# A spectral filter plus a gated MLP on one core: a task list by earliest positions, evacuations on ScalarE, one group's fix on VectorE, finer first loads, and down projections last

## The chip, the cores and the metric

The kernel runs on one core of a Trainium2 chip. The metric is the device time of one launch in microseconds (us), the median over several launches. Every run was also traced, so each has a *span* (first to last instruction), which is about 2 us shorter than the device time of the same run.

Runs that were sent together ran on one chip, interleaved with runs of the kernel before, and are compared with those. On chips 2 and 5 every kernel, the one before included, lost 10 to 18 us more in its first 31 us or so (the kernel before about 14 us, by its times). No number from such a chip is set against a number from another chip without saying so.

## The reference

```python
def reference(A_x, A_w_r, A_w_i, B_x, B_w_gate, B_w_up, B_w_down):   # B_x is not used
    x  = A_x                                  # [1, 2048, 512] bf16
    xn = layernorm(x)                         # over the 512 columns
    spec = irfft2(rfft2(xn) * (w_r + 1j*w_i)) # over 2048 x 512
    h    = gelu_tanh(xn @ w_gate) * (xn @ w_up)   # 512 -> 1792
    return x + spec + h @ w_down              # 1792 -> 512
```

Both transforms are done as matrix products. So TensorE has two streams of work: the gated MLP ("GLU": gate and up products, then down products), and a spectral chain of short steps, each of which this kernel copies out of PSUM before the next starts (such a copy of [128 x 512] takes 0.60 us on ScalarE in the changed kernel).

## The kernel before

The sequence is 16 chunks of 128 rows. GLU work comes in 56 units (4 blocks of 512 rows, 14 column slices). The spectral work is a list of tasks that are dealt out evenly between the units. The steps have short names, by the tile that they write: `tp` transposes of normalised x, `bp` first column step, `dp` row step, `ep` second column step, then the filter on VectorE, `gp` the inverse column step, `yp` the inverse row step, and `y_ps` the down products. A scheduler in the framework may move instructions a little within an engine's queue; the order used below is the one that the traces show.

The parts that matter here (cuts marked with `...`):

```python
def evac(o, i):                       # PSUM -> SBUF copies of bp, dp, gp
    flip[0] ^= 1
    if flip[0]: nc.scalar.copy(out=o, in_=i)
    else:       nc.vector.tensor_copy(out=o, in_=i)

def filt(g):                          # one of 8 groups
    V = nc.vector
    ...                               # ten VectorE operations, [128 x 512] or [128 x 1024], two of them [128 x 4] copies
    if g == 0:                        # one partition of group 0 needs a real-valued fix
        G = nc.gpsimd
        G.tensor_tensor(out=u[:, 0], in0=E0[:, :, 0], in1=TR0, op=ALU.mult)   # [1 x 512]
        ...                           # seven such operations, the last one tiny

def glu(sb, fc):
    ...                               # 4 gate and 4 up matmuls of 512 columns
    nc.scalar.activation(out=ge[:], in_=gp[:], func=AF.Gelu_apprx_tanh)
    nc.vector.tensor_tensor(out=hT[sb][:, fc, :], in0=up[:], in1=ge[:], op=ALU.mult)
    # gate and up PSUM tiles: two buffers each

layernorm(0)                          # chunks 0 to 3, rsqrt by 12 small VectorE operations
transposes(0)
tasks = []                            # ... layernorm, transposes, fold, bp for all chunks
for g in range(NG + 3):
    if g < NG:           tasks += [dstep(g, 0), dstep(g, 1)]      # as lambdas
    if 1 <= g < NG + 1:  tasks += [cstep(g - 1) and filt(g - 1)]
    if g >= 3:           tasks += [icstep(g - 3)]
# tasks dealt out evenly over 41 units; down(0..3) before unit 42, down(4..15) at the end
```

Of the kernel before, what the change touches and what calls it, by code (L numbers as in the profile page):

```python
# [10 lines left out]
P = 128  # L11
BF16 = mybir.dt.bfloat16
F32 = mybir.dt.float32
I32 = mybir.dt.int32
ALU = mybir.AluOpType
AF = mybir.ActivationFunctionType

S = 2048
D = 512
NC = 16  # L20
NG = 8
NE = 4
# [131 lines left out]
def kernel(  # L154
# [34 lines left out]
    Bs = pc.tile([P, 4, 2, NG, NC, 8], BF16, name="Bs", tag="Bs")  # L189
    RF_t = pc.tile([P, NC, P], BF16, name="RF_t", tag="RF")  # L190
    late = {}
    TR = pc.tile([P, NG, 2, 258], BF16, name="TR")
    TI = pc.tile([P, NG, 2, 258], BF16, name="TI")

    def cc(name, shape=None):
        o, w = ccols[name]
# [2 lines left out]
    def load_consts(first, last):  # L199
        a, b = ccols[first][0], sum(ccols[last])  # L200
        nc.sync.dma_start(out=CT[:, a:b], in_=cap[:, a:b])


    nc.sync.dma_start(out=x_t[:, 0:2, :], in_=x_v[:, 0:2, :])
    nc.sync.dma_start(out=x_t[:, 2:4, :], in_=x_v[:, 2:4, :])
    load_consts("ident", "ident")
    FCH = [(0, 256), (256, 768), (768, 1280), (1280, 1792)]
    fa, fb = FCH[0]
    nc.sync.dma_start(out=Wg_sb[:, :, fa:fb], in_=wg_v[:, :, fa:fb])
    nc.sync.dma_start(out=Wu_sb[:, :, fa:fb], in_=wu_v[:, :, fa:fb])  # L210
    nc.sync.dma_start(out=x_t[:, 4:8, :], in_=x_v[:, 4:8, :])
    nc.sync.dma_start(out=RF_t[:], in_=rf_d.rearrange("p (c k) -> p c k", c=NC))
    for fa, fb in FCH[1:]:
        nc.sync.dma_start(out=Wg_sb[:, :, fa:fb], in_=wg_v[:, :, fa:fb])
        nc.sync.dma_start(out=Wu_sb[:, :, fa:fb], in_=wu_v[:, :, fa:fb])
        if fa == 256:
            nc.sync.dma_start(out=x_t[:, 8:12, :], in_=x_v[:, 8:12, :])
            nc.sync.dma_start(out=x_t[:, 12:16, :], in_=x_v[:, 12:16, :])
            load_consts("F0", "F3")
    load_consts("I0", "M20")  # L220


# [23 lines left out]
    nc.gpsimd.memset(xn[:, :, D:D + 2], 0.0)  # L246


    def rsqrt(y, var):

        V = nc.vector
        v = pw.tile([P, 4], F32, name="v")
        t = pw.tile([P, 4], F32, name="t")
        V.tensor_scalar(out=v[:], in0=var, scalar1=EPS, scalar2=None, op0=ALU.add)
        vi, ti, yi = v[:].bitcast(I32), t[:].bitcast(I32), y[:].bitcast(I32)
        V.tensor_scalar(out=ti, in0=vi, scalar1=1, scalar2=None, op0=ALU.logical_shift_right)
        V.tensor_scalar(out=yi, in0=ti, scalar1=-1, scalar2=0x5F3759DF, op0=ALU.mult, op1=ALU.add)
        for _ in range(3):
            V.tensor_tensor(out=t[:], in0=y[:], in1=y[:], op=ALU.mult)
            V.scalar_tensor_tensor(out=t[:], in0=v[:], scalar=-0.5, in1=t[:],  # L260
                                   op0=ALU.mult, op1=ALU.mult)
            V.scalar_tensor_tensor(out=y[:], in0=t[:], scalar=1.5, in1=y[:],
                                   op0=ALU.add, op1=ALU.mult)

    def layernorm(cg):
        c0 = 4 * cg
        stats = pw.tile([P, 4, nc.vector.BN_STATS_DIM], F32, name="stats")
        mv = pw.tile([P, 4, nc.vector.BN_AGGR_DIM], F32, name="mv")
        rstd = pw.tile([P, 4], F32, name="rstd")
        for j in range(4):  # L270
            nc.vector.bn_stats(out=stats[:, j, :], in_=x_t[:, c0 + j, :])  # L271
            nc.vector.bn_aggr(out=mv[:, j, :], in_=stats[:, j, :])
        rsqrt(rstd, mv[:, :, 1])
        for j in range(4):
            nc.vector.tensor_scalar(out=xn[:, c0 + j, 0:D], in0=x_t[:, c0 + j, :],  # L275
                                    scalar1=mv[:, j, 0:1], scalar2=rstd[:, j:j + 1],
                                    op0=ALU.subtract, op1=ALU.mult)

    def transposes(cg):
        for h in range(2):  # L280
            c0 = 4 * cg + 2 * h
            tp = ps.tile([P, NE, 2, P], BF16, name="tp", tag="S", bufs=4)
            for e in range(NE):
                for j in range(2):
                    nc.tensor.transpose(tp[:, e, j, :], xn[:, c0 + j, e * P:(e + 1) * P], ident)  # L285
            if h == 0:
                nc.vector.tensor_copy(out=xnT[:, :, c0:c0 + 2, :], in_=tp[:])
            else:
                nc.scalar.copy(out=xnT[:, :, c0:c0 + 2, :], in_=tp[:])  # L289


    fold_out = {}
# [19 lines left out]
    def pstep(cg, q):  # L312
        xf = fold_out[cg]
        bp = ps.tile([P, 4, 2 * NG, 8], F32, name="bp", tag="S", bufs=4)
        for j in range(4):
            nc.tensor.matmul(bp[:, j], lhsT=xf[:, j, q, :], rhs=RF_t[:, 4 * cg + j, :],  # L316
                             start=True, stop=True)
        o = Bs[:, q].rearrange("p r g c a -> p c (r g) a")[:, 4 * cg:4 * cg + 4]
        evac(o, bp[:])

    flip = [0]

    def evac(o, i):
        flip[0] ^= 1
        if flip[0]:
            nc.scalar.copy(out=o, in_=i)
        else:
            nc.vector.tensor_copy(out=o, in_=i)

    ds_tiles = {}  # L330

# [41 lines left out]
    def filt(g):  # L373
# [21 lines left out]
        if g == 0:  # L395

            u = pw.tile([1, 2, 2, 256], BF16, name="u", bufs=1)
            G = nc.gpsimd
            E0, F0 = E[0:1], F[0:1]
            TR0, TI0 = TR[0:1, 0, :, 0:256], TI[0:1, 0, :, 0:256]  # L400
            G.tensor_tensor(out=u[:, 0], in0=E0[:, :, 0], in1=TR0, op=ALU.mult)
            G.tensor_tensor(out=u[:, 1], in0=E0[:, :, 1], in1=TI0, op=ALU.mult)
            G.tensor_tensor(out=F0[:, 0], in0=u[:, 0], in1=u[:, 1], op=ALU.add)
            G.tensor_tensor(out=u[:, 0], in0=E0[:, :, 1], in1=TR0, op=ALU.mult)
            G.tensor_tensor(out=u[:, 1], in0=E0[:, :, 0], in1=TI0, op=ALU.mult)
            G.tensor_tensor(out=F0[:, 1], in0=u[:, 0], in1=u[:, 1], op=ALU.subtract)
            G.tensor_tensor(out=F0[:, :, :, 0], in0=E0[:, :, :, 0].rearrange("p r s -> p s r"),  # L407
                            in1=f_tiles["t0"][:], op=ALU.mult)
# [49 lines left out]

    hT = {}

    def glu(sb, fc):
        if fc == 0:
            tag = ("hT0", "hT1", "xn", "hT0")[sb]
            hT[sb] = pc.tile([P, NFC, 512], BF16, name=f"hT{sb}", tag=tag)
        rhs = xnT[:, :, 4 * sb:4 * sb + 4, :].rearrange("p e c q -> p e (c q)")
        gp = ps.tile([P, 512], F32, name="g_ps", tag="G", bufs=2)
        up = ps.tile([P, 512], F32, name="u_ps", tag="U", bufs=2)
        for e in range(NE):
            nc.tensor.matmul(gp[:], lhsT=Wg_sb[:, e, fc * P:(fc + 1) * P], rhs=rhs[:, e, :],  # L469
                             start=(e == 0), stop=(e == NE - 1))  # L470
        for e in range(NE):
            nc.tensor.matmul(up[:], lhsT=Wu_sb[:, e, fc * P:(fc + 1) * P], rhs=rhs[:, e, :],  # L472
                             start=(e == 0), stop=(e == NE - 1))
        ge = pw.tile([P, 512], BF16, name="ge", bufs=3)
        nc.scalar.activation(out=ge[:], in_=gp[:], func=AF.Gelu_apprx_tanh)  # L475
        nc.vector.tensor_tensor(out=hT[sb][:, fc, :], in0=up[:], in1=ge[:], op=ALU.mult)  # L476

    def down(c):
        sb, cl = c // 4, c % 4
# [8 lines left out]
        nc.sync.dma_start(out=out_v[:, c, :], in_=y_sb[:])  # L488


    layernorm(0)
    transposes(0)
    tasks = []
    for cg in range(1, 4):
        tasks.append(lambda cg=cg: layernorm(cg))
        tasks.append(lambda cg=cg: transposes(cg))
    for cg in range(4):
        tasks.append(lambda cg=cg: fold(cg))
        for q in range(4):
            tasks.append(lambda cg=cg, q=q: pstep(cg, q))  # L500
    tasks.append(tables_fix)
    for g in range(NG + 3):
        if g < NG:
            tasks.append(lambda g=g: dstep(g, 0))
            tasks.append(lambda g=g: dstep(g, 1))
        if 1 <= g < NG + 1:
            tasks.append(lambda g=g: (cstep(g - 1), filt(g - 1)))
        if g >= 3:
            tasks.append(lambda g=g: icstep(g - 3))
    for c in range(NC):  # L510
        tasks.append(lambda c=c: idstep(c))
    units = [(sb, fc) for sb in range(NSB) for fc in range(NFC)]
    ti = 0
    SPAN = 41
    for i, u in enumerate(units):
        if i == 3 * NFC:
            while ti < len(tasks):
                tasks[ti]()
                ti += 1
            for c in range(4):  # L520
                down(c)
        glu(*u)
        target = (i + 1) * len(tasks) // SPAN
        while ti < min(target, len(tasks)):
            tasks[ti]()
            ti += 1
    for c in range(4, NC):
        down(c)


# [28 lines left out]
```

## Time and profile before

| | |
|---|---|
| device time | 209.67 us, median of 3 (209.47 to 210.68) |
| span of the profiled run | 208.9 us (a fourth run, which took 211.05 us) |
| TensorE busy | 187.7 us, 90% of the span |
| all matmuls at their full-speed spacing | about 180 us (an estimate) |
| first transpose / first gate matmul | 10.55 / 13.80 us |

The estimate in the fourth line takes the spacing that full-speed groups show in the timeline (about 0.060 us for 128 columns, 0.110 for 256, 0.216 for 512) times the number of matmuls. TensorE is therefore the engine that bounds the kernel, and what can be won is the time in which it stands still or runs slowly.

From the page of the kernel before: busy time of the engines, then the span in 40 slices of 5.2 us, then the chain of waits by engine.

```profile
span 208.9 us, 2903 instructions
...
PE 187.7 (90%) x1040; PEld 94.3 (45%) x1040; DVE 140.3 (67%) x360; ACT 71.5 (34%) x118; POOL 30.3 (15%) x41
...
PE   0079999999999199999999999999999999999992
...
DVE  2998999999779979999995999323433312212121
...
PEclk9999999999999759999999999999999999999998
...
PE 74%; DVE 13%; POOL 3%; DMA 3%; issue 2%; ACT 2%; SPq 1%; POOLq 0%; DVEq 0%
```

The PE row has two holes: the first two slices and slice 14 (about 68 to 73 us), and the granted clock dips just there and after. VectorE (DVE) is almost full until about 130 us, with a dip at 110 to 115 us, and 10 to 40% busy after that.

The waits of TensorE in the kernel before, longest first: who waited for whom, us in total, times, longest.

```profile
PE tp L285 <- DVE xn L275: 10.6, 1, 10.6
PE gp L422 <- POOL F L407: 4.8, 1, 4.8
PE g_ps L469 <- ACT xnT L289: 1.1, 1, 1.1
PE gp L422 <- DVE F L393: 0.4, 1, 0.4
```

The timeline of TensorE around the second hole, in the kernel before: start, duration of the group, instructions, and in brackets the idle time before it with what ended it.

```profile
72.56 1.89 PE L422 MATMUL gp<-CT,F 128*128 128x256 bf16 x8 [4.84 <-POOL F L407]
74.24 0.74 PE L336 MATMUL dp<-CT,Bs 128*128 128x129 bf16 x4
74.78 1.91 PE L469 MATMUL g_ps<-xnT,Wg_sb 128*128 128x512 bf16 x4
...
79.09 1.03 PE L469 MATMUL g_ps<-xnT,Wg_sb 128*128 128x512 bf16 x4
```

Four gate matmuls of the same shape take 1.91 us after the hole and 1.03 us about four microseconds later (the record of a group ends after the next group has started, at 80.12 against 79.95 us for the later one, so read starts: 74.78 to 76.48 is 1.70 us, 79.09 to 79.95 in the same trace is 0.86 us). TensorE ran at half speed after the pause: the clock records of the packed trace put it at half speed from 70.84 to 77.67 us. The windows view says the same: busy times of the engines, then the granted clock, DMA share, GB/s.

```profile
56.00:68.00 12.00, 11.71 (x65) 5.58 (x62) 9.86 (x19) 6.17 (x11) 4.36 (x4) 1.00 0.01 3
68.00:78.00 10.00, 5.44 (x22) 2.84 (x23) 8.92 (x16) 3.34 (x6) 4.35 (x4) 0.66 0.00 0
```

What TensorE waited for is POOL (GpSimd), at work on one single partition. And while POOL works, some of VectorE's operations take longer (1.59 instead of 0.68 us for the one below). Timeline of POOL in the kernel before, one of its operations on a single partition:

```profile
67.72 1.64 POOL L404 TENSOR_TENSOR u<-E,TR 1x512 bf16<-1x512 bf16 x1
```

And the timeline of VectorE in the same kernel, one line of it, the same [128 x 1024] multiply for two groups:

```profile
62.08 0.68 DVE L386 TENSOR_TENSOR m_746<-X,TI 128x1024 bf16<-128x1024 bf16 x1
...
68.32 1.59 DVE L386 TENSOR_TENSOR m_818<-X,TI 128x1024 bf16<-128x1024 bf16 x1
```

The multiply at 68.32 us, beside POOL, took 1.59 us; the one at 62.08, alone, 0.68 us. The slow one ended at 69.91 us, after POOL's operation had ended at 69.36.

### The profile page before, as it was taken

To read this page: it belongs to the slowest core of one execution; us is meant where nothing else is said; L and a number is where in the kernel's file an instruction comes from. 1 tells how busy PE (TensorE), PEld (TensorE's weight loads), DVE (VectorE), ACT (ScalarE), POOL (GpSimd) and SP (SyncE) were. 2 spreads that over 40 slices of the span, in tenths; PEclk is the share of its full clock that TensorE was granted. 3 is DMA by queue.
4 is the path that set the end of the run, shared out by engine and by line. 5 is a ranking of instruction groups with operands and counts; after the bars stand their busy time and mean duration, and the time that the engine had idled before them with its cause. 6 is when DMAs were issued, how large, how long until landed. Compare 5 with 4: busy or idle time off the path is not lost.

```text
span 208.9 us, 2903 instructions
## 1 busy us (share of the span) xinstructions
PE 187.7 (90%) x1040; PEld 94.3 (45%) x1040; DVE 140.3 (67%) x360; ACT 71.5 (34%) x118; POOL 30.3 (15%) x41
## 2 busy tenths in 40 slices
PE   0079999999999199999999999999999999999992
PEld 0043544654554055554555555444444444444440
DVE  2998999999779979999995999323433312212121
ACT  2042434653663335665635775002333300000000
POOL 3777761000043800000000000000000000000000
PEclk9999999999999759999999999999999999999998
DMA  5999976900200000000000000032000002221320
GB/s 150 358 376 340 341 175 160 306 0 3 100 0 6 0 0 0 0 3 0 0 0 2 3 0 0 29 100 75 0 0 0 3 25 79 78 96 53 102 68 32
DMA packets 14718, 16.00 MB, mean 77 GB/s; under 512 B 1472, under 2 KB 13392, under 8 KB 14704
## 3 DMA queue, kind: packets, MB, share of 16 engines
q1 hardware_dynamic: 14096, 14.62, 22.2%
q0 software_dynamic: 608, 1.19, 1.9%
q8 instruction: 8, 0.13, 0.2%
q14 instruction: 6, 0.05, 0.1%
HBM read 13.71 MB, written 2.10 MB: 76 GB/s over the span
## 4 chain that ended last, share of the span: by engine, by line
PE 74%; DVE 13%; POOL 3%; DMA 3%; issue 2%; ACT 2%; SPq 1%; POOLq 0%; DVEq 0%
PE y_ps L482 23%; PE g_ps L469 19%; PE u_ps L472 18%; PE gp L422 3%; DMA x_t<-in_A_x_dram 3%; PE yp L439 2%; PE tp L285 2%; PE dp L336 2%; PE bp L316 2%; PE y_ps L484 2%; DVE hT_177 L476 2%; DVE stats L271 1%; DVE xn L275 1%; ACT xnT L289 1%; DVE hT_1133 L476 1%
## 5 line engine op out<-in xcount | busy, mean ns | idle before, releaser
L469 PE MATMUL g_ps<-xnT,Wg_sb 128*128 128x512 bf16 x224 | 61.5, 392 | 1.1 <-ACT xnT L289 1.1
L472 PE MATMUL u_ps<-xnT,Wu_sb 128*128 128x512 bf16 x224 | 60.3, 388 | 0.0
L475 ACT ACTIVATE ge<-g_ps 128x512 bf16<-128x512 f32 x56 | 33.5, 598 | 55.0 <-PE g_ps L469 54.6
L487 DVE TENSOR_TENSOR y_sb<-y_ps,y_sb 128x512 bf16<-128x512 f32 x16 | 11.1, 691 | 39.2 <-PE y_ps L484 39.2
L472 PEld LDWEIGHTS <-Wu_sb 128*128 128x128 bf16 x224 | 22.3, 100 | 27.2 <-issue 3.9
L469 PEld LDWEIGHTS <-Wg_sb 128*128 128x128 bf16 x224 | 21.7, 100 | 23.1 <-issue 3.5
L476 DVE TENSOR_TENSOR hT_1677<-u_ps,ge 128x512 bf16<-128x512 f32 x14 | 9.7, 692 | 14.6 <-PE u_ps L472 14.6
L285 PE MATMUL tp<-CT,xn 128*128 128x128 bf16 x64 | 6.3, 242 | 10.8 <-DVE xn L275 10.6
L422 PE MATMUL gp<-CT,F 128*128 128x256 bf16 x64 | 9.2, 290 | 5.3 <-POOL F L407 4.8
L354 ACT CAST E<-ep 128x512 bf16<-128x512 f32 x16 | 10.7, 735 | 8.7 <-PE ep L353 5.4
L271 DVE BATCH_NORM_STATS2 stats<-x_t 128x6 f32<-128x512 bf16 x16 | 10.6, 674 | 3.8 <-DMA x_t<-in_A_x_dram 3.7
L482 PE MATMUL y_ps<-Wd_sb,hT_177 128*128 128x512 bf16 x56 | 12.7, 379 | 0.0
L482 PE MATMUL y_ps<-Wd_sb,hT_633 128*128 128x512 bf16 x56 | 12.7, 379 | 0.0
L482 PE MATMUL y_ps<-Wd_sb,hT_1133 128*128 128x512 bf16 x56 | 12.7, 379 | 0.0
L482 PE MATMUL y_ps<-Wd_sb,hT_1677 128*128 128x512 bf16 x56 | 12.7, 379 | 0.0
L476 DVE TENSOR_TENSOR hT_633<-u_ps,ge 128x512 bf16<-128x512 f32 x14 | 9.5, 682 | 2.2 <-PE u_ps L472 2.2
L285 PEld LDWEIGHTS <-xn 128*128 128x128 bf16 x64 | 4.6, 108 | 13.0 <-DVE xn L275 12.6
L422 PEld LDWEIGHTS <-F 128*128 128x128 bf16 x64 | 6.3, 103 | 8.6 <-POOL F L407 5.3
L476 DVE TENSOR_TENSOR hT_177<-u_ps,ge 128x512 bf16<-128x512 f32 x14 | 9.5, 680 | 0.6 <-PE u_ps L472 0.6
L445 ACT CAST yf<-yp 128x512 bf16<-128x512 f32 x16 | 8.5, 591 | 4.1 <-PE yp L439 2.9
L476 DVE TENSOR_TENSOR hT_1133<-u_ps,ge 128x512 bf16<-128x512 f32 x14 | 9.5, 680 | 0.0
L236 POOL DMA_INDIRECT TR<-in_A_w_r_dram,idx_t x9 | 8.7, 971 | 5.0 <-DMA idx_t<-spec_rows 2.6
(108 smaller groups left out, 222.3 us busy)
## 6 DMA issues: line engine op xcount, KB each, us to landing
y_sb<-in_A_x_dram SPq DMA_DIRECT2D x16, 128.0 KB, 2.2
out_dram<-y_sb SPq DMA_DIRECT2D x16, 128.0 KB, 1.7
Wd_sb<-in_B_w_down_dram SPq DMA_DIRECT2D x1, 1792.0 KB, 8.1
x_t<-in_A_x_dram SPq DMA_DIRECT2D x3, 512.0 KB, 10.0
Wg_sb<-in_B_w_gate_dram SPq DMA_DIRECT2D x3, 512.0 KB, 11.2
Wu_sb<-in_B_w_up_dram SPq DMA_DIRECT2D x3, 512.0 KB, 10.7
CT<-spec_consts SPq DMA_DIRECT2D x1, 640.2 KB, 12.0
x_t<-in_A_x_dram SPq DMA_DIRECT2D x2, 256.0 KB, 3.0
```

The lines of the kernel that those rows point to most:

```text
L236: nc.gpsimd.indirect_dma_start(out=T[:, g, s, 0:W], out_offset=None, in_=w_in[:, :], in_offset=bass.IndirectOffsetOnAxis(ap=idx_t[:, g, s: ...
L271: nc.vector.bn_stats(out=stats[:, j, :], in_=x_t[:, c0 + j, :])
L285: nc.tensor.transpose(tp[:, e, j, :], xn[:, c0 + j, e * P:(e + 1) * P], ident)
L354: nc.scalar.copy(out=E[:, r].rearrange("p s (k t) -> p t s k", t=2), in_=ep[:].rearrange("p (t s k) -> p t s k", t=2, s=2))
L422: nc.tensor.matmul(gp[:, s], lhsT=F[:, s, r, t::2], rhs=cc(f"M{r + 1}" + z), start=(s == 0 and r == 0), stop=(s == 1 and r == 1), skip_gro ...
L445: nc.scalar.copy(out=yf[:, c % 2], in_=yp[:].rearrange("p (t k) -> p t k", t=2))
L469: nc.tensor.matmul(gp[:], lhsT=Wg_sb[:, e, fc * P:(fc + 1) * P], rhs=rhs[:, e, :], start=(e == 0), stop=(e == NE - 1))
L472: nc.tensor.matmul(up[:], lhsT=Wu_sb[:, e, fc * P:(fc + 1) * P], rhs=rhs[:, e, :], start=(e == 0), stop=(e == NE - 1))
L475: nc.scalar.activation(out=ge[:], in_=gp[:], func=AF.Gelu_apprx_tanh)
L476: nc.vector.tensor_tensor(out=hT[sb][:, fc, :], in0=up[:], in1=ge[:], op=ALU.mult)
L482: nc.tensor.matmul(y_ps[:], lhsT=hT[sb][:, f, cl * P:(cl + 1) * P], rhs=Wd_sb[:, f, :], start=(f == 0), stop=False)
L487: nc.vector.tensor_tensor(out=y_sb[:], in0=y_ps[:], in1=y_sb[:], op=ALU.add)
```

## The change

Its intent: start TensorE earlier, take work from VectorE, and place each spectral step by a list of earliest positions, so that no step is reached before its input can be ready. The diff, cut to its core (left out: two table tiles become one, whose space the last block's GLU result takes, now that all down projections come last):

```diff
 # loads: x first in two single chunks on two queues, weights in slices 256/384/576/576
-    nc.sync.dma_start(out=x_t[:, 0:2, :], in_=x_v[:, 0:2, :])
-    ...
+    load_x(0, 1); load_x(1, 1, nc.scalar); load_consts("ident", "ident"); load_x(2, 2, nc.scalar)
+    load_w(0, 256); load_w(256, 640); load_x(4, 4); load_w(640, 1216); load_x(8, 4); ...
 # layernorm of n chunks; the first two calls use ScalarE's square root
+        if c0 < 4:
+            nc.scalar.activation(out=rstd[:], in_=mv[:, :, 1], func=AF.Sqrt, bias=eps_t[:], scale=1.0)
+            nc.vector.reciprocal(out=rstd[:], in_=rstd[:])
+        else:
+            rsqrt(rstd, mv[:, :, 1], n)
 # copies of transposed x: all on VectorE (half were on ScalarE)
+        nc.vector.tensor_copy(out=xnT[:, :, c0:c0 + 2, :], in_=tp[:])
 # spectral evacuations: all on ScalarE
-        flip[0] ^= 1
-        if flip[0]: nc.scalar.copy(out=o, in_=i)
-        else:       nc.vector.tensor_copy(out=o, in_=i)
+        nc.scalar.copy(out=o, in_=i)
 # the one-partition fix of group 0
-            G = nc.gpsimd
+            G = nc.vector
 # the first block's 14 column slices as 28 half-width units (two chunks, 256 columns)
+    units = [(0, 2, fc) for fc in range(3)]
+    for fc in range(NFC):
+        units.append((2, 2, fc))
+        if fc + 3 < NFC: units.append((0, 2, fc + 3))
 # tasks with earliest positions, in us of GLU work (1.724 us per full unit)
+    for cg in range(4):
+        t = 8 + 5 * cg
+        tasks.append((t, fold(cg)));  tasks += [(t + 2 + q, pstep(cg, q)) for q in range(4)]
+    for g in range(NG):
+        t = 32 + 5.0 * g
+        tasks += [(t, dstep(g, 0)), (t + 1, dstep(g, 1)), (t + 4, cstep(g)), (t + 4, filt(g)), (t + 11, icstep(g))]
+    for c in range(NC): tasks.append((82 + 0.9 * c, idstep(c)))
 # all down projections after the last unit (four were before unit 42)
```

More of the change, by code (lines that the diff above doesn't have):

```diff
@@ L191 @@
     late = {}
-    TR = pc.tile([P, NG, 2, 258], BF16, name="TR")
-    TI = pc.tile([P, NG, 2, 258], BF16, name="TI")
+    TW = pc.tile([P, 2, NG, 2, 258], BF16, name="TW", tag="TW")
+    TR, TI = TW[:, 0], TW[:, 1]
     def cc(name, shape=None):
@@ L201, in load_consts, with load_x, load_w @@
         nc.sync.dma_start(out=CT[:, a:b], in_=cap[:, a:b])
-    nc.sync.dma_start(out=x_t[:, 0:2, :], in_=x_v[:, 0:2, :])
-    nc.sync.dma_start(out=x_t[:, 2:4, :], in_=x_v[:, 2:4, :])
-    load_consts("ident", "ident")
-    FCH = [(0, 256), (256, 768), (768, 1280), (1280, 1792)]
-    fa, fb = FCH[0]
-    nc.sync.dma_start(out=Wg_sb[:, :, fa:fb], in_=wg_v[:, :, fa:fb])
-    nc.sync.dma_start(out=Wu_sb[:, :, fa:fb], in_=wu_v[:, :, fa:fb])
-    nc.sync.dma_start(out=x_t[:, 4:8, :], in_=x_v[:, 4:8, :])
-    nc.sync.dma_start(out=RF_t[:], in_=rf_d.rearrange("p (c k) -> p c k", c=NC))
-    for fa, fb in FCH[1:]:
-        nc.sync.dma_start(out=Wg_sb[:, :, fa:fb], in_=wg_v[:, :, fa:fb])
-        nc.sync.dma_start(out=Wu_sb[:, :, fa:fb], in_=wu_v[:, :, fa:fb])
-        if fa == 256:
-            nc.sync.dma_start(out=x_t[:, 8:12, :], in_=x_v[:, 8:12, :])
-            nc.sync.dma_start(out=x_t[:, 12:16, :], in_=x_v[:, 12:16, :])
-            load_consts("F0", "F3")
+    def load_x(c0, n, eng=nc.sync):
+        eng.dma_start(out=x_t[:, c0:c0 + n, :], in_=x_v[:, c0:c0 + n, :])
+    def load_w(a, b):
+        nc.sync.dma_start(out=Wg_sb[:, :, a:b], in_=wg_v[:, :, a:b])
+        nc.sync.dma_start(out=Wu_sb[:, :, a:b], in_=wu_v[:, :, a:b])
+    load_x(0, 1)
+    load_x(1, 1, nc.scalar)
+    load_consts("ident", "ident")
+    load_x(2, 2, nc.scalar)
+    load_w(0, 256)
+    load_w(256, 640)
+    load_x(4, 4)
+    load_w(640, 1216)
+    load_x(8, 4)
+    nc.sync.dma_start(out=RF_t[:], in_=rf_d.rearrange("p (c k) -> p c k", c=NC))
+    load_w(1216, 1792)
+    load_x(12, 4)
+    load_consts("F0", "F3")
     load_consts("I0", "M20")
@@ L246, with rsqrt @@
     nc.gpsimd.memset(xn[:, :, D:D + 2], 0.0)
-    def rsqrt(y, var):
+    eps_t = pc.tile([P, 1], F32, name="eps_t")
+    nc.vector.memset(eps_t[:], EPS)
+    def rsqrt(y, var, n):
         V = nc.vector
-        v = pw.tile([P, 4], F32, name="v")
-        t = pw.tile([P, 4], F32, name="t")
+        v = pw.tile([P, n], F32, name="v")
+        t = pw.tile([P, n], F32, name="t")
         V.tensor_scalar(out=v[:], in0=var, scalar1=EPS, scalar2=None, op0=ALU.add)
@@ L263, in rsqrt, with layernorm @@
                                    op0=ALU.add, op1=ALU.mult)
-    def layernorm(cg):
-        c0 = 4 * cg
-        stats = pw.tile([P, 4, nc.vector.BN_STATS_DIM], F32, name="stats")
-        mv = pw.tile([P, 4, nc.vector.BN_AGGR_DIM], F32, name="mv")
-        rstd = pw.tile([P, 4], F32, name="rstd")
-        for j in range(4):
+    def layernorm(c0, n):
+        stats = pw.tile([P, n, nc.vector.BN_STATS_DIM], F32, name="stats")
+        mv = pw.tile([P, n, nc.vector.BN_AGGR_DIM], F32, name="mv")
+        rstd = pw.tile([P, n], F32, name="rstd")
+        for j in range(n):
             nc.vector.bn_stats(out=stats[:, j, :], in_=x_t[:, c0 + j, :])
             nc.vector.bn_aggr(out=mv[:, j, :], in_=stats[:, j, :])
-        rsqrt(rstd, mv[:, :, 1])
-        for j in range(4):
+        if c0 < 4:
[3 more added lines that the diff above has]
+            rsqrt(rstd, mv[:, :, 1], n)
+        for j in range(n):
             nc.vector.tensor_scalar(out=xn[:, c0 + j, 0:D], in0=x_t[:, c0 + j, :],
@@ L277, in layernorm, with transposes @@
                                     op0=ALU.subtract, op1=ALU.mult)
-    def transposes(cg):
-        for h in range(2):
-            c0 = 4 * cg + 2 * h
-            tp = ps.tile([P, NE, 2, P], BF16, name="tp", tag="S", bufs=4)
-            for e in range(NE):
-                for j in range(2):
-                    nc.tensor.transpose(tp[:, e, j, :], xn[:, c0 + j, e * P:(e + 1) * P], ident)
-            if h == 0:
-                nc.vector.tensor_copy(out=xnT[:, :, c0:c0 + 2, :], in_=tp[:])
-            else:
-                nc.scalar.copy(out=xnT[:, :, c0:c0 + 2, :], in_=tp[:])
+    def transposes(c0):
+        tp = ps.tile([P, NE, 2, P], BF16, name="tp", tag="S", bufs=4)
+        for e in range(NE):
+            for j in range(2):
+                nc.tensor.transpose(tp[:, e, j, :], xn[:, c0 + j, e * P:(e + 1) * P], ident)
+        nc.vector.tensor_copy(out=xnT[:, :, c0:c0 + 2, :], in_=tp[:])
     fold_out = {}
@@ L319, in pstep @@
         evac(o, bp[:])
-    flip = [0]
     def evac(o, i):
-        flip[0] ^= 1
-        if flip[0]:
-            nc.scalar.copy(out=o, in_=i)
-        else:
-            nc.vector.tensor_copy(out=o, in_=i)
+        nc.scalar.copy(out=o, in_=i)
     ds_tiles = {}
@@ L459, with glu @@
     hT = {}
-    def glu(sb, fc):
-        if fc == 0:
-            tag = ("hT0", "hT1", "xn", "hT0")[sb]
+    def glu(c0, n, fc):
+        sb, o, w = c0 // 4, (c0 % 4) * P, n * P
+        if sb not in hT:
+            tag = ("hT0", "hT1", "xn", "TW")[sb]
             hT[sb] = pc.tile([P, NFC, 512], BF16, name=f"hT{sb}", tag=tag)
-        rhs = xnT[:, :, 4 * sb:4 * sb + 4, :].rearrange("p e c q -> p e (c q)")
-        gp = ps.tile([P, 512], F32, name="g_ps", tag="G", bufs=2)
-        up = ps.tile([P, 512], F32, name="u_ps", tag="U", bufs=2)
+        rhs = xnT[:, :, c0:c0 + n, :].rearrange("p e c q -> p e (c q)")
+        gp = ps.tile([P, w], F32, name="g_ps", tag="G", bufs=2)
+        up = ps.tile([P, w], F32, name="u_ps", tag="U", bufs=2)
         for e in range(NE):
@@ L473, in glu @@
                              start=(e == 0), stop=(e == NE - 1))
-        ge = pw.tile([P, 512], BF16, name="ge", bufs=3)
+        ge = pw.tile([P, w], BF16, name="ge", bufs=3)
         nc.scalar.activation(out=ge[:], in_=gp[:], func=AF.Gelu_apprx_tanh)
-        nc.vector.tensor_tensor(out=hT[sb][:, fc, :], in0=up[:], in1=ge[:], op=ALU.mult)
+        nc.vector.tensor_tensor(out=hT[sb][:, fc, o:o + w], in0=up[:], in1=ge[:], op=ALU.mult)
     def down(c):
@@ L488, in down @@
         nc.sync.dma_start(out=out_v[:, c, :], in_=y_sb[:])
-    layernorm(0)
+    layernorm(0, 2)
     transposes(0)
-    tasks = []
+    units = [(0, 2, fc) for fc in range(3)]
+    for fc in range(NFC):
+        units.append((2, 2, fc))
+        if fc + 3 < NFC:
+            units.append((0, 2, fc + 3))
+    for sb in range(1, NSB):
+        units += [(4 * sb, 4, fc) for fc in range(NFC)]
+    tasks = [(0, lambda: layernorm(2, 2)), (0, lambda: transposes(2))]
     for cg in range(1, 4):
-        tasks.append(lambda cg=cg: layernorm(cg))
-        tasks.append(lambda cg=cg: transposes(cg))
+        t = 4 + 6 * (cg - 1)
+        tasks.append((t, lambda cg=cg: layernorm(4 * cg, 4)))
+        tasks.append((t + 3, lambda cg=cg: transposes(4 * cg)))
+        tasks.append((t + 3, lambda cg=cg: transposes(4 * cg + 2)))
@@ L497 @@
     for cg in range(4):
-        tasks.append(lambda cg=cg: fold(cg))
+        t = 8 + 5 * cg
+        tasks.append((t, lambda cg=cg: fold(cg)))
         for q in range(4):
-            tasks.append(lambda cg=cg, q=q: pstep(cg, q))
-    tasks.append(tables_fix)
-    for g in range(NG + 3):
-        if g < NG:
-            tasks.append(lambda g=g: dstep(g, 0))
-            tasks.append(lambda g=g: dstep(g, 1))
-        if 1 <= g < NG + 1:
-            tasks.append(lambda g=g: (cstep(g - 1), filt(g - 1)))
-        if g >= 3:
-            tasks.append(lambda g=g: icstep(g - 3))
@@ L510 @@
-    for c in range(NC):
-        tasks.append(lambda c=c: idstep(c))
-    units = [(sb, fc) for sb in range(NSB) for fc in range(NFC)]
-    ti = 0
-    SPAN = 41
-    for i, u in enumerate(units):
-        if i == 3 * NFC:
-            while ti < len(tasks):
-                tasks[ti]()
-                ti += 1
-            for c in range(4):
-                down(c)
-        glu(*u)
-        target = (i + 1) * len(tasks) // SPAN
-        while ti < min(target, len(tasks)):
-            tasks[ti]()
-            ti += 1
@@ L527 @@
-    for c in range(4, NC):
+            tasks.append((t + 2 + q, lambda cg=cg, q=q: pstep(cg, q)))
+    tasks.append((20, tables_fix))
+    t0, dt = 32, 5.0
+    for g in range(NG):
+        tasks.append((t0 + dt * g, lambda g=g: dstep(g, 0)))
+        tasks.append((t0 + dt * g + 1, lambda g=g: dstep(g, 1)))
+        tasks.append((t0 + dt * g + 4, lambda g=g: cstep(g)))
+        tasks.append((t0 + dt * g + 4, lambda g=g: filt(g)))
+        tasks.append((t0 + dt * g + 11, lambda g=g: icstep(g)))
@@ L528 @@
+    t0, dt = 82, 0.9
+    for c in range(NC):
+        tasks.append((t0 + dt * c, lambda c=c: idstep(c)))
+    tasks.sort(key=lambda x: x[0])
+    ti, now = 0, 0.0
+    for u in units:
+        while ti < len(tasks) and tasks[ti][0] <= now:
+            tasks[ti][1]()
+            ti += 1
+        glu(*u)
+        now += 1.724 * u[1] / 4
+    while ti < len(tasks):
+        tasks[ti][1]()
+        ti += 1
+    for c in range(NC):
         down(c)
```

## The prediction

> **What bounds it now.** TensorE. The page has PE busy 187.7 of 208.9 us, and the chain of waits is 74% PE. With the timeline's warm matmul spacing (512 columns 0.216 us, 256 columns 0.110, 128 columns about 0.065), all matmuls need about 180.6 us (an estimate). The first transpose starts at 10.55 us, the last matmul ends near 205.0: about 14 us in between are lost, and 3.9 us of tail follow. By timeline and chain:
> - about 5 us at the start: the first gate matmul waits until 13.80 us for transposed x, and the array runs at half speed until about 20 us;
> - 4.84 us, the longest PE wait during the work, at 67.7 to 72.6: the first inverse-column matmul waits for one-partition operations on POOL (1.2 to 1.6 us each); then PE runs at half speed until about 77.5 (granted clock 0.66 in 68 to 78 us by windows), another 2.6 us. [...] (0.427 us per 512-column matmul instead of 0.216);
> - about 2 us in small waits on DVE, which is 35.06 of 36 us busy in 20 to 56 us.
>
> **What changes.**
> 1. Start. Two chunks instead of four are normalised first, and ScalarE's square root replaces eleven chained DVE operations (6.51 to 9.58 us). First transpose near 7, first gate matmul near 9 to 9.5. The half-speed phase stays, about 3 us. Gain 4 to 5 us.
> 2. Group 0's fix moves to DVE: seven operations of about 0.35 us, and the inverse step is scheduled 7 us of GLU time after the filter. The wait and the re-warming go: 7 to 7.5 us. DVE also loses the stretching it shows beside POOL (a multiply 1.59 instead of 0.68, a copy 1.01 instead of 0.16)[...].
> 3. Evacuations. 24 casts leave DVE (0.60 each, 14 us); DVE takes all transpose copies (+2.7) and split multiplies (+1). ACT grows from 71.5 to about 81 us, harmless. DVE falls to about 124 us.
> 4. Early DVE work stays dense. Adding up DVE durations in program order against PE's, DVE is still 3 to 4 us late around the last half-width units (about 37 to 46 us); before, it cost 1 to 2. This returns about 2 us.
> 5. Downs last, half-width matmuls, finer loads: about neutral. Tail unchanged, 3.9 us.
>
> **Sum.** First gate matmul 9.2 us, less 1 of transposes already done, plus 180.8 of matmuls, 3 half-speed, 3.5 DVE waits, 3.9 tail: 199.4 us span; time about 200.3 us. Range 197.0 to 204.5. Faster by over 2%: 0.93; within 2%: 0.06; slower: 0.01.
>
> **What would show it.** No PE wait over 1 us after 50 us; no POOL line in the chain after the loads; granted clock near 1.0 from about 17 us; gate matmuls from about 9 us; PE busy near 183 us, DVE 124, ACT 81; remaining PE gaps between 30 and 46 us ending in a DVE multiply.
>
> **What would make it wrong.** The load of chunks 4 to 7 now follows 1.3 MB of weights: a DVE queue stuck on it holds back the second transpose copy. ACT as sole evacuator, in order with the gelus, could block PE through the four shared PSUM buffers. Denser DVE starvation early[...] would bring 203 to 205. No DVE stall at all would give about 196.5.

The sum: 9.2 - 1 + 180.8 + 3 + 3.5 + 3.9 = 199.4 us. "Warm" in this text is the spacing of 0.216 us for 512 columns, "re-warming" the half speed that the clock records show from 70.84 to 77.67 us. "Warm-up" in an expectation below is the half speed at the start (6.91 to 10.84 us in the changed kernel); the words say nothing of a cause.

## The result

The changed kernel took 201.34 us (median of 4, 200.97 to 202.15) against 209.57 us for the kernel before on the same chip. The ratio is 0.960, with a 95% interval of 0.956 to 0.965. Ratios in this text are the mean time of one kernel's fast runs over that of the other's of the same rounds, so not quite the ratio of the medians that are quoted. Chip 12, also undisturbed, gave 201.12 against 210.69 us, ratio 0.956.

The page of the changed kernel, the same lines as before:

```profile
span 199.2 us, 3152 instructions
...
PE 182.9 (92%) x1135; PEld 103.8 (52%) x1152; DVE 127.9 (64%) x352; ACT 82.7 (42%) x154; POOL 21.8 (11%) x34
...
PE   0579999789999999999999999999999999999992
...
DVE  3899999999427987687697693599942121212121
...
PEclk9999999999999999999999999999999999999999
...
PE 75%; DVE 14%; issue 3%; DMA 3%; SPq 1%; ACT 1%; DVEq 0%
```

The hole at slice 14 is gone, POOL is no longer in the chain, and TensorE starts one slice earlier. New is a weak spot in slice 8 (35 to 40 us). The waits of TensorE in the changed kernel:

```profile
PE tp L293 <- DVE xn L285: 6.9, 1, 6.9
PE u_ps L472 <- DVE hT_172 L476: 3.5, 4, 1.4
PE gp L421 <- DVE F L406: 0.6, 1, 0.6
PE g_ps L469 <- DVE xnT L294: 0.2, 1, 0.2
```

And the places of the new wait in the timeline of TensorE: an up product needs a PSUM buffer that VectorE has not yet emptied.

```profile
9.21 1.01 PE L469 MATMUL g_ps<-xnT,Wg_sb 128*128 128x256 bf16 x4 [0.20 <-DVE xnT L294]
...
14.03 0.60 PE L472 MATMUL u_ps<-xnT,Wu_sb 128*128 128x256 bf16 x4 [1.37 <-DVE hT_172 L476]
...
37.77 1.03 PE L472 MATMUL u_ps<-xnT,Wu_sb 128*128 128x256 bf16 x8 [1.30 <-DVE hT_172 L476]
...
40.20 0.60 PE L472 MATMUL u_ps<-xnT,Wu_sb 128*128 128x256 bf16 x4 [0.53 <-DVE hT_172 L476]
```

The inverse step that had waited 4.84 us for POOL now waits 0.62 us for VectorE and runs at full speed:

```profile
69.96 1.05 PE L421 MATMUL gp<-CT,F 128*128 128x256 bf16 x8 [0.62 <-DVE F L406]
```

The window that showed the half speed before, now in the changed kernel (full clock, 9.32 us of 10 busy):

```profile
68.00:78.00 10.00, 9.32 (x57) 5.20 (x57) 8.08 (x22) 6.38 (x12) 0.00 (x0) 1.00 0.01 2
```

### A table of lost time

The two kernels run their steps in a different order, so equal times of the clock can't be compared. What can be compared is the *lost time* of TensorE at a milestone: the time at which the first matmul of a step starts, minus the full-speed time of all matmuls ahead of it in the queue. It is worked out from the start times in the traces and from the order of instructions, with the spacings given above. These are rounded, so a figure is good to about 0.3 us.

```
lost us at the first matmul of    gate    bp     dp     gp     yp    end
before                           12.84  16.24  16.73  21.99  25.48  25.71
changed                           8.25  11.17  14.89  15.66  15.70  15.83
difference                       -4.59  -5.07  -1.84  -6.33  -9.78  -9.88
```

"End" is the end of the last down product. The first gate matmul came 4.6 us earlier, but at the first row step (`dp`, 52.5 us before and 55.7 us changed) only 1.8 us of that were left. From there to the end the old kernel lost 9.0 us and the new one 0.9 us: this stretch gives 8.0 of the 9.9 us. The table compares the two profiled runs, and that of the kernel before took 211.05 us, 1.5 us above its median; the medians differ by 8.2 us. Where that run lost the 1.5 us is not known.

### The profile page after: what moved, and what is told of

It is laid out like the page before. It is cut to its first block, busy times and chain, and to the rows that moved or that the text cites. A ratio compares the mean times of both kernels' runs of the same rounds, so it can differ in the third digit from the quotient of the medians.

```text
span 199.2 us, 3152 instructions
## 1 busy us (share of the span) xinstructions
PE 182.9 (92%) x1135; PEld 103.8 (52%) x1152; DVE 127.9 (64%) x352; ACT 82.7 (42%) x154; POOL 21.8 (11%) x34
## 4 chain that ended last, share of the span: by engine, by line
PE 75%; DVE 14%; issue 3%; DMA 3%; SPq 1%; ACT 1%; DVEq 0%
PE y_ps L482 24%; PE u_ps L472 19%; PE g_ps L469 17%; PE gp L421 4%; DMA x_t<-in_A_x_dram 3%; DVE hT_172 L476 3%; PE yp L438 2%; DVE stats L277 2%; PE dp L335 2%; PE y_ps L484 2%; PE ep L351 1%; PE bp L321 1%; PE ep L352 1%; PE tp L293 1%; DVE xnT L294 1%
## 5 line engine op out<-in xcount | busy, mean ns | idle before, releaser
L472 PE MATMUL u_ps<-xnT,Wu_sb 128*128 128x512 bf16 (+1 forms) x277 | 59.9, 338 | 3.9 <-DVE hT_172 L476 3.5
L469 PE MATMUL g_ps<-xnT,Wg_sb 128*128 128x512 bf16 (+1 forms) x271 | 59.5, 337 | 0.5 <-DVE xnT L294 0.2
L475 ACT ACTIVATE ge<-g_ps 128x512 bf16<-128x512 f32 (+1 forms) x70 | 36.0, 514 | 31.8 <-PE g_ps L469 22.8
L472 PEld LDWEIGHTS <-Wu_sb 128*128 128x128 bf16 x280 | 27.5, 98 | 26.3 <-issue 5.1
L476 DVE TENSOR_TENSOR hT_804<-u_ps,ge 128x512 bf16<-128x512 f32 x14 | 9.6, 686 | 7.5 <-PE u_ps L472 5.8
L476 DVE TENSOR_TENSOR hT_1579<-u_ps,ge 128x512 bf16<-128x512 f32 x14 | 9.6, 686 | 5.5 <-PE u_ps L472 5.5
L482 PE MATMUL y_ps<-Wd_sb,hT_804 128*128 128x512 bf16 x55 | 12.7, 379 | 0.1
L482 PE MATMUL y_ps<-Wd_sb,hT_1579 128*128 128x512 bf16 x55 | 12.7, 379 | 0.1
L482 PE MATMUL y_ps<-Wd_sb,hT_172 128*128 128x512 bf16 x55 | 12.7, 379 | 0.1
L476 DVE TENSOR_TENSOR hT_1172<-u_ps,ge 128x512 bf16<-128x512 f32 x14 | 9.7, 689 | 3.0 <-PE u_ps L472 2.4
L476 DVE TENSOR_TENSOR hT_172<-u_ps,ge 128x256 bf16<-128x256 f32 x28 | 11.4, 411 | 0.1
L327 ACT CAST ds<-dp 128x512 bf16<-128x512 f32 x16 | 9.5, 597 | 4.4 <-PE dp L335 4.4
L327 ACT CAST Bs<-bp 128x512 bf16<-128x512 f32 x16 | 8.5, 597 | 6.7 <-PE bp L321 6.7
L327 ACT CAST Gs<-gp 128x512 bf16<-128x512 f32 x16 | 8.6, 592 | 3.3 <-PE gp L421 3.3
L240 POOL DMA_INDIRECT TW<-in_A_w_r_dram,idx_t x9 | 8.7, 967 | 5.5 <-DMA idx_t<-spec_rows 3.1
```

The lines of the kernel that those rows point to most:

```text
L240: nc.gpsimd.indirect_dma_start(out=T[:, g, s, 0:W], out_offset=None, in_=w_in[:, :], in_offset=bass.IndirectOffsetOnAxis(ap=idx_t[:, g, s: ...
L469: nc.tensor.matmul(gp[:], lhsT=Wg_sb[:, e, fc * P:(fc + 1) * P], rhs=rhs[:, e, :], start=(e == 0), stop=(e == NE - 1))
L472: nc.tensor.matmul(up[:], lhsT=Wu_sb[:, e, fc * P:(fc + 1) * P], rhs=rhs[:, e, :], start=(e == 0), stop=(e == NE - 1))
L476: nc.vector.tensor_tensor(out=hT[sb][:, fc, o:o + w], in0=up[:], in1=ge[:], op=ALU.mult)
L482: nc.tensor.matmul(y_ps[:], lhsT=hT[sb][:, f, cl * P:(cl + 1) * P], rhs=Wd_sb[:, f, :], start=(f == 0), stop=False)
```

## The experiments

Theory: the later stretch is won by taking the fix of group 0 from POOL, because that removes a wait (4.84 us), a half-speed stretch (70.84 to 77.67 us) and a slowdown of VectorE (1.59 instead of 0.68 us for a multiply) at once; the early gain is mostly given back, because up to about 50 us VectorE sets the pace (in the kernel before it is busy 35.06 of the 36 us from 20 to 56 us). Rivals: the list of positions, or the relief of VectorE by ScalarE's evacuations, does it.

### 1. The kernel before, only the fix moved to VectorE (`b_fix_dve`, repeated as `b_fix_dve_2`)

```diff
-            G = nc.gpsimd
+            G = nc.vector
```

> The kernel before with one word changed: group 0's seven one-partition operations run on DVE instead of POOL. Theory (the removed POOL wait is worth 7 us by itself): the 4.84 us wait of the first inverse-column matmul and the half-speed stretch after it vanish, time 202 to 204 us. Rival (the new schedule is needed, because DVE is already full there): the 2.5 us of added DVE work turns into another PE wait of 2 to 4 us, time 205 to 208 us.

> The kernel before with group 0's fix on VectorE, again, on another chip: on the first one every kernel lost over 13 us near the start. Theory: ratio to the kernel before 0.965 to 0.97, that is 203 to 204 us on a chip where the kernel before takes 210, and the loss of PE between the first row step and the first inverse row step falls from 8.75 to about 2 us, as it did there.

Measured: 216.94 us against 223.95 for the kernel before, ratio 0.969 (0.966 to 0.972); repeated on another chip 215.98 against 223.32, ratio 0.967 (0.961 to 0.973). Both chips were of the disturbed kind, so the absolute expectation (202 to 204 us) can't be checked there, but the difference can: 7.0 and 7.3 us, as the theory said. The wait that was 4.84 us is now, in the first of the two runs:

```profile
81.55 1.05 PE L422 MATMUL gp<-CT,F 128*128 128x256 bf16 x8 [0.51 <-DVE F L407]
```

The matmuls behind it run at full speed at once (1.05 us for the group that took 1.89). The lost time from `dp` to `yp` falls from 8.75 us (kernel before, undisturbed chip) to 2.07 and 2.07 us. One changed word gives most of what the whole change gives in this stretch, without the list of positions.

### 2. The kernel before, POOL kept, the inverse step later (`b_later`)

```diff
-        if g >= 3: tasks.append(lambda g=g: icstep(g - 3))
+        if g >= 5: tasks.append(lambda g=g: icstep(g - 4))    # ahead of cstep/filt of this round
+        if g == 5: tasks.append(lambda: icstep(0))            # group 0: about four units later
-        F = pw.tile(..., name="F", bufs=3)
+        F = pw.tile(..., name="F" if g else "Fz", bufs=3 if g else 1)   # Y: one buffer, to make room
```

> The kernel before with group 0's operations still on POOL, but the inverse step of group 0 moved about four GLU units later and that of group 1 one unit. Theory (what hurts is a PE wait at a fixed place, so distance alone cures it): no PE wait over 1.5 us near 70 us, time 202 to 205 us. Rival ([...]DVE is what limits this stretch): the wait moves to DVE, time 206 to 209 us.

Measured: 221.96 us against 223.95, ratio 0.991 (0.988 to 0.995): 2.0 us, the rival's range. No matmul of the spectral chain waits for POOL any more, but TensorE then waits six times, 5.0 us in all: five times for VectorE, once for ScalarE. Two of them:

```profile
83.56 1.02 PE L472 MATMUL u_ps<-xnT,Wu_sb 128*128 128x512 bf16 x4 [0.68 <-DVE hT L476]
...
86.09 0.38 PE L353 MATMUL ep<-ds,CT 128*128 128x512 bf16 x1 [1.29 <-DVE ds L328]
```

VectorE in the same run shows what held it up; six of its operations beside POOL's (71.8 to 74.3 and 79.1 to 85.5 us) are stretched, others are not:

```profile
79.67 1.01 DVE L379 COPY X<-E 128x4 bf16<-128x4 bf16 x1
80.72 0.69 DVE L385 TENSOR_TENSOR m<-X,TR 128x1024 bf16<-128x1024 bf16 x1
81.33 1.58 DVE L386 TENSOR_TENSOR m<-X,TI 128x1024 bf16<-128x1024 bf16 x1
...
87.97 0.16 DVE L379 COPY X<-E 128x4 bf16<-128x4 bf16 x1
```

The copy took 1.01 us beside POOL and 0.16 us afterwards. VectorE's busy time is 139.8 us here and 136.4 us with the fix moved, although the latter includes 2.1 to 2.6 us for the fix itself (six operations of 0.41 us and one of 0.16, which overlap a little). So POOL's seven operations cost VectorE about 5 to 6 us (an estimate); adding up the delays of the stretched operations in the timeline gives about 5 us. So distance alone cures the wait but not the loss. I had expected the opposite.

### 3. The changed kernel with the fix back on POOL (`a_fix_pool`)

```diff
-            G = nc.vector
+            G = nc.gpsimd
```

> The changed kernel with group 0's seven operations put back on POOL. In the changed kernel the first inverse-column matmul still waited 0.62 us for DVE, so the new schedule leaves no slack. Theory: POOL's longer operations (1.2 to 1.6 us against about 0.35) bring back a wait of 3 to 6 us and a half-speed stretch, time 205 to 209 us. Rival (the schedule's distance covers it): within 1 us of the changed kernel, 201 to 202 us.

Measured: 226.88 us, slower than the kernel before (223.95) on the same chip, ratio 1.013 (1.006 to 1.020). The chip was disturbed and the unedited changed kernel was not run on it, so the time gives no difference to that kernel; the lost time does. (Before its first `bp` this kernel lost 18 us more than the changed kernel does on the undisturbed chip, where the variants of the kernel before lost 11.5 to 13.5 us more than that kernel. So a whole time on these chips also holds a disturbance of its own size.) From `dp` to `yp` it is 7.74 us against 0.81 us in the changed kernel, 6.9 us more, in the expected range of 4 to 8. From `bp` to `dp` it is 3.64 us against 3.72: the undisturbed parts agree between the chips. The wait:

```profile
92.92 1.89 PE L421 MATMUL gp<-CT,F 128*128 128x256 bf16 x8 [4.39 <-POOL F L406]
```

The list of earliest positions had given group 0 eleven us of GLU work from row step to inverse step, and that was just enough with VectorE (0.62 us of wait) and not enough with POOL. So the list alone does not win the stretch, and experiment 1 wins it without the list.

### 4. The changed kernel with alternating evacuations (`a_flip`)

```diff
-        nc.scalar.copy(out=o, in_=i)
+        flip[0] ^= 1
+        if flip[0]: nc.scalar.copy(out=o, in_=i)
+        else:       nc.vector.tensor_copy(out=o, in_=i)
```

> The changed kernel with spectral evacuations alternating between ScalarE and VectorE as before. Theory (DVE limits the stretch of 30 to 50 us): eight more casts of 0.6 us there lengthen the PE waits for DVE multiplies from about 2 to 5 or 6 us, time 203.5 to 206 us. Rival (DVE has slack over the whole): within 1 us of the changed kernel.

Measured: 221.79 us on the disturbed chip; again the lost time has to tell. From `bp` to `dp` it is 6.63 us against 3.64 us in `a_fix_pool` on the same chip and 3.72 us in the changed kernel: 3.0 us more, in the expected range of 2 to 5. From `dp` to the end it is 1.0 us against 0.9: there VectorE has room. The single wait that grew, to 3.12 us, was followed by half speed (eight 256-column matmuls in 1.86 us instead of 1.03):

```profile
57.81 1.86 PE L478 MATMUL u_ps<-xnT,Wu_sb 128*128 128x256 bf16 x8 [3.12 <-DVE hT L482]
```

### 5. The changed kernel unedited, and with the old start (`after_again`, `a_old_start`)

```diff
 # a_old_start: loads as in the kernel before, and
+    layernorm(0, 4)        # four chunks together, rsqrt on VectorE
+    transposes(0); transposes(2)
+    units = [(0, 4, fc) for fc in range(NFC)]      # full width
```

> The changed kernel, unedited, as the reference of this call, because in the first experiments all kernels, the one before too, lost about 14 us near the start on that chip. If that loss belongs to the chip and not to the kernels, this call shows either the first ratio again (0.960) or, on such a chip, about 0.98.

> The changed kernel with the old start: loads in the old order, four chunks normalised together with the chained VectorE operations, full-width first units; schedule, evacuations and the rest as changed. Theory (the earlier first gate matmul is a gain of its own): 3 to 5 us slower than the unedited changed kernel of the same call. Rival (VectorE limits the stretch of 30 to 50 us and starts at 3.4 us either way, so PE's earlier start is mostly given back there): 0 to 2 us slower.

On an undisturbed chip: 201.12 us for the changed kernel, 202.79 us with the old start (ratios to the kernel before 0.956 and 0.964). The old start costs 1.7 us by the medians, the rival's range. In the profiled runs (for the old start its fastest, 201.44 us) the first gate matmul comes at 14.02 us against 9.51, yet the lost time at `dp` is 15.56 against 14.92. The wait list of the old start has no wait for `hT` at all, only these two after the first transpose:

```profile
PE g_ps L472 <- DVE xnT L297: 0.8, 1, 0.8
PE gp L424 <- DVE F L409: 0.6, 1, 0.6
```

Starting TensorE 4.5 us earlier mostly made it lose time later, 3.4 us of it in waits for VectorE's multiplies.

### 6. Full-width first units (`a_full_first`) and copies of transposed x on ScalarE (`a_relief2`)

```diff
 # a_full_first
+    layernorm(2, 2); transposes(2)
-    units = [(0, 2, fc) for fc in range(3)] ; ...        # half-width, interleaved
+    units = [(0, 4, fc) for fc in range(NFC)]
 # a_relief2
-        nc.vector.tensor_copy(out=xnT[:, :, c0:c0 + 2, :], in_=tp[:])
+        if c0 >= 2: nc.scalar.copy(out=xnT[:, :, c0:c0 + 2, :], in_=tp[:])
+        else:       nc.vector.tensor_copy(out=xnT[:, :, c0:c0 + 2, :], in_=tp[:])
```

> The changed kernel with full-width first units (all four chunks transposed before the first gate matmul), new loads and square root kept. Theory (half-width units buy about 1.5 us of earlier start): first gate matmul near 11 us and 1 to 2 us slower. Rival (half-width units also cost VectorE 1.1 us of extra multiplies in its limiting stretch): within 0.7 us.

> The changed kernel with the copies of transposed x of chunks 2 to 15 on ScalarE instead of VectorE (seven copies, 0.60 us each, 4.1 us off VectorE). Theory (VectorE limits the stretch of 30 to 50 us and holds the third unit at 12.7 to 14.0 us): the four PE waits for VectorE multiplies, 3.5 us in all, shrink to below 1.5 us, and the kernel is 1.5 to 3 us faster than the unedited changed kernel of the same call. Rival (ScalarE, in order with the gelus, then holds PE instead): no faster.

Measured: 200.87 and 200.51 us against 201.12 us; ratios to the kernel before 0.956, 0.954 and 0.956, with overlapping intervals. Full width: no difference, the rival's outcome. The first gate matmul comes at 11.80 us instead of 9.51, and again nothing is lost by it.

The relief missed my expectation of 1.5 to 3 us. Its mechanism was right, its worth was not. The waits of TensorE with relief:

```profile
PE u_ps L475 <- DVE hT L479: 0.8, 2, 0.6
PE g_ps L472 <- ACT ge L478: 0.7, 3, 0.4
```

Waits for VectorE multiplies fell from 3.4 us (in `after_again`) to 0.8, but 0.7 us of waits for ScalarE came up, and the half-speed phase at the start ended about 1.5 us later in this run (a group of four 256-column matmuls still took 0.85 us at 11.03 us, where the changed kernel ran at full speed from about 10.9). What remains of the early loss are many gaps below 0.2 us that the wait list does not attribute. About 4 us taken from VectorE brought the first row step only 0.5 us forward (55.15 instead of 55.69 us), so VectorE is not all that holds this stretch.

### 7. The kernel before with the evacuations alone, and with both edits (`b_act_evac`, `b_two`)

```diff
 # both
-        flip[0] ^= 1 ...                 # alternate
+        nc.scalar.copy(out=o, in_=i)
 # b_two also
-            G = nc.gpsimd
+            G = nc.vector
```

> The kernel before with all spectral evacuations on ScalarE, POOL kept. Theory (the POOL wait is what counts, and relief of VectorE does not touch it): the POOL wait stays at 3 us or more and the gain is 1 to 3 us, from the early stretch and the later small waits. Rival (a saturated VectorE is the common cause of both): the POOL wait falls below 1.5 us and the gain is over 5 us.

> The kernel before with only these two edits: all spectral evacuations on ScalarE and group 0's fix on VectorE; old start, old task order, old places of the down projections. Theory (the new task list and the new start are worth little once VectorE is relieved): 201 to 203 us, at most 2 us behind the changed kernel, ratio to the kernel before 0.957 to 0.967. Rival (the list of earliest positions is a gain of its own): 204 us or more.

Disturbed chip. The evacuations alone: 221.88 against 223.32 us, ratio 0.995 (0.990 to 1.001), not clear of zero. The POOL wait stays at 3.81 us:

```profile
83.29 1.89 PE L418 MATMUL gp<-CT,F 128*128 128x256 bf16 x8 [3.81 <-POOL F L403]
```

Both edits: 215.91 us, ratio 0.968 (0.964 to 0.972), the same as the fix alone in that call (0.967). That is just outside the range I expected by ratio (0.957 to 0.967), but its interval reaches into it. From `dp` to the end the lost time is 1.7 us with both, 2.2 us with the fix alone, 7.1 us with the evacuations alone. For the early stretch this chip can't speak: TensorE and VectorE stood still there for other reasons, and VectorE's backlog was hidden. So whether the two edits alone reach the changed kernel on an undisturbed chip is open.

### 8. Full-width first units and relief together (`a_full_relief`)

The edits are those of 6, both at once.

> The changed kernel with full-width first units and the copies of transposed x of chunks 2 to 15 on ScalarE. Each alone gave 0.3 to 0.6 us; together the first gate matmul no longer waits behind the load of chunks 4 to 7 (11.8 to about 10 us) and VectorE has 5 us less work than in the changed kernel in the early stretch. Theory (VectorE still limits there): 198.5 to 200 us. Rival (what is left is half-speed warm-up and waits for ScalarE): 200.5 us or more.

Measured on the disturbed chip: 211.06 us against 223.32, ratio 0.948 (0.944 to 0.953); 4.9 us faster than `b_two` and 4.9 us faster than the fix alone. The absolute expectation can't be checked there. From `bp` to `dp` it loses 0.85 us, against 3.72 us in the changed kernel and 3.64 us in `a_fix_pool` on a disturbed chip; from `dp` to the end 0.9 us, as the changed kernel. But full width alone (`a_full_first`) already loses only 1.3 us from `bp` to `dp`, because its loss lies ahead of `bp`, and it was no faster than the changed kernel. So this stretch does not show a gain. It beats the kernel before by 5.2% on that chip, which no other kernel did on any chip. Part of that can be the disturbance: ahead of `bp` it lost about 10 us more than `a_full_first` on the undisturbed chip, where the variants of the kernel before lost 11.5 to 13.5 us more. It was not run beside the changed kernel on one chip, so by how much it beats that one is open.

### The disturbed chips

Chips 2 and 5 showed it, in all runs of all kernels. TensorE, ScalarE and VectorE were mostly idle together until about 31 us, though matmuls whose results ScalarE had to read were done: in `b_two` the second group of gate matmuls started at 19.04 us, and its activation at 30.71 us. ScalarE's timeline in `b_two`, where "remote" is a release by something that the profile does not show:

```profile
17.69 0.60 ACT L471 ACTIVATE ge<-g_ps 128x512 bf16<-128x512 f32 x1 [0.65 <-issue]
30.71 1.09 ACT L471 ACTIVATE ge<-g_ps 128x512 bf16<-128x512 f32 x2 [12.42 <-remote]
```

The DMA rows move as many bytes as on the undisturbed chips, with about the same number of packets. But the packed traces from chips 2 and 5 hold only 747 to 850 records of landed transfers instead of 1317 to 1344, and 1709 to 1815 semaphore records of the engines instead of 2322 to 2391. So what an engine waited for is less sure in these traces, and the cause of the disturbance is open.

## Why the prediction was right, point by point

- **Span.** Predicted 199.4 us, measured 199.2. The time was 1.0 us above the 200.3 predicted because I took 0.9 us for what lies outside the span, from the median time minus the profiled span; but the profiled run of the kernel before had itself taken 211.05 us, so the difference was 2.1 us. The profiled run of the changed kernel has 1.8 us.
- **POOL ("7 to 7.5 us").** Right: one word changed gave 7.0 and 7.3 us. One part had no size in the prediction: it named the stretching of VectorE beside POOL, which is about 5 us, and without getting that back a longer distance gives only 2.0 us (experiment 2). In the whole change the stretch from the first row step on gives 8.0 us.
- **Start ("gain 4 to 5 us") and the return ("about 2 us").** The first gate matmul came at 9.21 us (9.2 predicted), and 4.6 us were gained there. The chain of small operations that ScalarE's square root replaced has twelve links in the trace, not eleven. The return was mis-sized: 2.75 us instead of 2, measured at the first row step, which leaves 1.8 us. Undoing the start (experiment 5) costs only 1.7 us in time and 0.6 us in lost time.
- **Half speed ("3") and waits for VectorE ("3.5").** The waits were 3.5 us in sum, but 1.37 us of them at 12.7 to 14.0 us, not "between 30 and 46 us": there VectorE had been held by the load of chunks 4 to 7 (a DMA wait of 1.29 us until 10.45 us, then mostly the statistics of these chunks until the multiply at 13.57 us), which had been named as a danger. The half-speed phase was over near 10.9 us, about 1 us of loss after the first gate matmul instead of 3. Small gaps of about 2.4 us, which I had not in the sum, took its place. With 0.6 us of wait at 70 us, 7.6 us were lost after the first gate matmul instead of 6.5. Against that, the matmuls need about 179.5 us by the spacings above instead of 180.8, mostly because I took 0.065 us for 128 columns instead of 0.060. So terms of about 1 to 2 us were off and cancelled: that the span came within 0.2 us is in part luck.
- **What would show it.** PE 182.9 (183 predicted), ACT 82.7 (81), DVE 127.9 (124); no POOL in the chain; no TensorE wait over 0.62 us after 50 us. These came as written, VectorE's busy time least. The gaps "between 30 and 46 us" were there too, with 2.1 of the 3.5 us.
- **"All downs last, half-width, finer loads: about neutral."** Half-width is neutral (experiment 6). Down projections last and the finer loads were not tested alone.

What the points on half speed and POOL rest on, as measured: waits of 4.84 (kernel before), 4.39 (`a_fix_pool`), 3.81 (`b_act_evac`) and 3.12 us (`a_flip`) were followed by half speed (eight 256-column matmuls in 1.86 to 1.89 us), waits of 1.37 and 1.30 us in the changed kernel were not (four in 0.60 us, eight in 1.03). A VectorE multiply beside POOL's work took 1.59 us instead of 0.68. POOL's [1 x 512] operations took 1.21 to 1.64 us in the kernel before, with VectorE running beside them, the same operations on VectorE 0.41 us (`b_fix_dve`), so 3 to 4 times less; how long they take on POOL alone no run shows.

## What to carry to other kernels

When a fast engine waits for a slow one, look also at what the slow one does to the third: POOL's work on one partition took 4.8 us of TensorE in the wait, about 2.6 us in the half speed after it (an estimate, half of the 5.1 us from 72.56 to 77.67), and about 5 us of VectorE (the estimate of experiment 2), so that moving the work paid 7 us and moving the wait 2 us. Before shortening a start, find the engine that sets the pace behind it: of 4.6 us gained here at the first matmul 1.8 us arrived at the first row step. VectorE was part of that, as more work for it cost 3.0 us there (experiment 4); but less work for it gained only about 0.6 us (experiment 6), so what else sets the pace until 50 us is open. A schedule can be compared across reorderings by lost time at milestones, which here also agreed between chips, for stretches after the disturbance, where plain times did not. But it has to be followed to the end: a schedule can move a loss ahead of a milestone without removing it (experiment 8).

## What else the traces show of half speed

- At the start of the kernel before, from the first transpose at 10.55 us to 19.64 us (with a gap of 1.1 us in it), the matmuls have half-speed spacing, 0.427 us for 512 columns; in the changed kernel from 6.91 to 10.84 us, 0.21 us for 256 columns. About 4 us were lost, 1.9% of the span, and about 1.7 us (estimates, half of the time that TensorE worked there).
- In the kernel before, half speed began at 70.84 us, 3.1 us after TensorE had stopped at 67.72. How long a wait must be for half speed to follow is not shown.
- The profile's row of granted clock shows 1.00 before the first clock record, which comes at 19.64 us in the kernel before and at 10.84 us in the changed one, although the matmuls until then have half-speed spacing; the spacing has to be read.
